# Retention, Mish layer and GLU layer on one core: the planner knows the port that VectorE and GpSimd share and uses longer durations, activations stay in PSUM banks until they are split, and one pair's first chunk is multiplied out plainly

## Chip, core and metric

The kernel runs on one core of a Trainium2 chip. The metric is the device time of one execution in microseconds (us); lower is better. TensorE (PE) does the matrix products, VectorE (DVE), ScalarE (ACT) and GpSimd (POOL) do the elementwise work, and SyncE (SP) issues the loads and stores.

## What is computed

Three stages follow each other: a retention over 768 steps (16 pairs of batch and head), a feed-forward layer with the activation h*tanh(softplus(h)) (Mish), and a gated layer (GLU). All inputs are float32.

```python
def _attn_ref(q, k, v):
    ...
    for t in range(S):
        state = gamma[None, :, None, None] * state + np.einsum('bhd,bhe->bhde', k[:, :, t], v[:, :, t])
        y[:, :, t] = scale * np.einsum('bhd,bhde->bhe', q[:, :, t], state)
...
def _moe_ref(x, w_in, w_out):       # x 1536x512, w_in 512x2048, w_out 2048x512
    h = x @ w_in
    sp = np.where(h > 20.0, h, np.log1p(np.exp(np.minimum(h, 20.0))))
    g = h * np.tanh(sp)
    return (g @ w_out).astype(np.float32)
...
def _moe2_ref(x, w_gate, w_val, w_out):     # 512x1536, 512x1536, 1536x512
    gate = 1.0 / (1.0 + np.exp(-(x @ w_gate)))
    val = x @ w_val
    return (gate * val @ w_out).astype(np.float32)
```

## The kernel before

**Tiles.** The 1536 tokens are three chunks of 512 (c = 0, 1, 2). Activations lie feature by token: `acc_t[c]` holds four 128x512 tiles of chunk c in SBUF. Every float32 factor is written as the sum of a rounded high part and a low part (`split`, L269: ACT writes the high part, another engine subtracts it to get the low part), and a product of two factors is three matmuls (`mm3`, L287). A weight arrives by DMA as 64-bit words and is decoded by two ACT and two DVE operations (`decode`, L273: tiles `raw` and `v`), then split into a ring (`ww`, `wo`, `wq`).

**Products.** The hidden features of a layer come in pairs. For a pair, chunks 1 and 2 are not multiplied by the weights with eight block products but with seven, from sums of blocks (`pair_steps`, L489; `main_steps`; steps p1 to p7, each six matmuls of 512 columns into PSUM tile `h`). Chunk 0 gets the same scheme on its two halves (`side_steps`: six matmuls of 256 columns a step, PSUM tile `hx`). The block sums of the activations are formed once a layer by `sums_of` (L452): `T1` to `T4` for chunks 1 and 2 (tiles `T`, `t`), `YT1` to `YT3` and parts of `xc` for chunk 0 (tiles `YT`, `t`); `B` are unsummed blocks. Between products DVE adds partial results (`u<-h,s`, `u<-h,u`, `h<-h,u`, the same with `hx`). `plain_steps` (L578) is the unreduced product: 4 blocks by 3 matmuls of 512 columns for each of the two feature groups; the kernel uses it for the first pairs of a layer, whose sums are not ready.

**Activation.** In layer 1 `mish` (L598) has ACT write Mish of a PSUM bank into an SBUF tile `e`; in layer 2 `gate` (L603) has ACT write the sigmoid into `e`, and `glu` (L608) has DVE multiply the value's bank into `e`. `put_g` (L593) then splits `e` into `g`: ACT the high part, and for the low part `lo_eng["g"]`, which is POOL or, by the planner's choice, DVE (L836).

**Second product of a layer.** `o1` and `o2` multiply `g` by `wo` into PSUM tiles `o` (two banks, L612: only the first call uses `h` banks), and DVE adds each to `acc` (`acc<-o,acc`; the first one of a layer is an ACT copy `acc<-o`). There are eight PSUM banks: four `h`, two `o`, two `hx`.

**Order.** Until `early.clear()` (L831) instructions are issued as written. After it every call makes a `Node` (L112), and `replay` (L168) lists them all: the PE instructions stay in the written order (`chain`), every other engine's order comes from a walk in time. A node's rank is its own cost plus the longest way from it to the end; an idle engine takes the ready node of highest rank, unless that would hold up a later node of higher rank. Costs are functions of the element count (L161 to L165), the time from one engine's end to another's start is `lag`. `either` (L166) marks operations that POOL or DVE may do; before, DVE takes one only when POOL would be too late for it (L221). The engines then execute these fixed lists, each waiting on semaphores. `three` (L695) interleaves main steps, side steps and `o` tiles on PE.

Of the kernel before, what the change touches and what calls it, by code (L numbers as in the profile page):

```python
# [23 lines left out]
def kernel(ctx, tc, qk, nv, w1i, w1o, w2g, w2v, w2o, ma_in, og_in, sg_in, ck_in, out):  # L24
# [28 lines left out]
    early = [True]  # L53
    WIDTH = {F32: 4, F32R: 4, I32: 4, I64: 8, U8: 1}
# [57 lines left out]
    class Node:  # L112


        def __init__(self, queues, name, kw):
# [3 lines left out]
            self.cost = [q.cost(big.at.size, kw) for q in queues]  # L119
# [40 lines left out]

    pe = Queue(nc.tensor, lambda n, kw: (kw["rhs"].at.size + 32) / 2400, 0.2)  # L161
    dve = Queue(nc.vector, lambda n, kw: (0.157 + 0.00104 * n) * (1 if psum(kw) else 1.3), 0.1)
    act = Queue(nc.scalar, lambda n, kw: 0.17 + 0.0009 * min(n, N), 0.1)
    pool = Queue(nc.gpsimd, lambda n, kw: 0.08 + 0.00258 * n, 0.1)
    sync = Queue(nc.sync, lambda n, kw: 3.3 if isinstance(kw["out"], Part) else 1.6, 0.3)  # L165
    either = Either(pool, dve)  # L166

    def replay():  # L168
# [22 lines left out]

        def lag(m, n):
            return 0 if m.queues[0] is n.queues[0] else m.queues[0].lag
# [4 lines left out]
        late = 0  # L198
        free = {q: 0.0 for q in (pe, dve, act, pool, sync)}
        wait = {n: len(n.after) for n in nodes}  # L200
        line = {q: [] for q in free}
        done = []

        def enter(n):
            n.ready = max((m.end + lag(m, n) for m in n.after), default=0.0)
            for q in n.queues:
                line[q].append(n)

        for n in nodes:
            if not wait[n]:  # L210
                enter(n)
        now = 0.0
        while len(done) < len(nodes):
            moved = False
            for q in free:
                if free[q] > now or not line[q]:
                    continue
                pick = None
                for n in sorted((n for n in line[q] if n.ready <= now), key=lambda n: -n.rank):
                    cost = n.cost[n.queues.index(q)]  # L220
                    if len(n.queues) > 1 and q is dve:  # L221
                        if max(now, free[pool]) + n.cost[0] <= whole + late - n.rank + n.cost[0]:
                            continue
                    end = now + cost
                    if any(u.rank > n.rank and u.ready < end and end > max(u.ready, whole + late - u.rank)
                           and u.ready > now and len(u.queues) == 1 for u in line[q]):
                        continue
                    pick = n
                    break
                if not pick:  # L230
                    continue
                n = pick
                n.start, n.end, n.queue = now, now + n.cost[n.queues.index(q)], q
                free[q] = n.end
                late = max(late, n.start - (whole - n.rank)) if q is pe else late
                for k in n.queues:
                    line[k].remove(n)
                done.append(n)
                moved = True
                for m in n.then:  # L240
                    wait[m] -= 1
                    if not wait[m]:
                        enter(m)
            if not moved:
                later = [t for t in free.values() if t > now] + [n.ready for q in free for n in line[q] if n.ready > now]
                now = min(later)
# [47 lines left out]
    G0 = 4  # L294
    I0 = G0 // 2
    pieces = [("w1i", f) for f in range(G0)] + [("w1o", f) for f in range(G0)]
# [40 lines left out]
    def direct(key):  # L337
        return key[1] == 1 and key[2] < I0 or key[1] == 2 and key[2] < 2

# [112 lines left out]
    def sums_of(x0, x1, bt, cols, eng):  # L452
# [3 lines left out]
        def form(n, k, in0, in1, to=None):  # L456
            if to is None:
                to = (up if cols == N else upv).tile([P, cols], F32, tag="u", name="t")
            eng.tensor_tensor(out=to, in0=in0, in1=in1, op=ALU.subtract)
# [12 lines left out]
        for k in range(2):  # L472
            steps.append(lambda k=k: form("T4", k, x0[:, 2 + k], t["T2", k], t["T2", k]))
# [5 lines left out]
    def side_sums():  # L479
        return sums_of(acc_t[0][:, :, :H], acc_t[0][:, :, H:], y_t, H, pool if early else either)  # L480
# [97 lines left out]
    def plain_steps(key, done, halves=None, own=False):  # L578

        def one(i):  # L580
            o = hx["pool"].tile([P, N], F32, tag=f"x{i}", name="hx") if own and i in hx["own"] else hbank()
            w = weight(("a", *key, i))
            for kk in range(KK):
                xs, k = (xc_t, kk) if not halves else (b_t[halves[kk // 2]], kk % 2)
                mm3(o, lambda a: w[:, a, kk * P:kk * P + P], lambda b: xs[:, k, b, :], kk == 0, kk == KK - 1)
            spend(("a", *key, i))
            r[i] = o
            done(i, r)

        r = {}  # L590
        return [lambda: one(0), lambda: one(1)]

    def put_g(e, key):  # L593
        g = gp.tile([P, 2, N], F32R, tag="g", name="g")
        split(e, g[:, 0], g[:, 1], lo_eng["g"])
        g_t[key] = g
# [337 lines left out]
```

## Time and profile before

| | |
|---|---|
| median of 3 runs | 592.2 us (592.03 to 592.25) |
| the profiled execution | 592.67 us |
| its span, first to last instruction | 590.5 us |
| PE, DVE, ACT, POOL busy | 98%, 66%, 50%, 68% |

The profiled execution lies 0.47 us above the median, and 2.17 us of it lie outside the span. PE's busy time counts a running matmul as busy, so 98% doesn't say that nothing is lost: a matmul's recorded length overlaps the next one's, and a short wait can hide in that. What PE loses is read from the start times of its products: each has a fixed number of matmuls, and the distance to the next start shows whether PE went on at its own pace.

### The profile page before, as it was taken

The numbers are of one execution on the slowest core, as the hardware profiler recorded it, in microseconds if no ns is written. First come the engines' busy times: TensorE is split into PE (matmuls) and PEld (weight loads), VectorE is DVE, ScalarE is ACT, GpSimd is POOL, SyncE is SP. The second block draws the span as 40 slices with busy tenths as digits, with TensorE's granted clock in tenths as the row PEclk, the third lists the DMA queues.
The fourth block names the chain that finished last, engine by engine and source line by source line (L and its number), as shares of the span: only waits on it lengthen the run. The fifth ranks groups of instructions, "written<-read, shape, count | busy, mean of one in ns | idle before, by whom it ended". The sixth has DMA issues, their size and how long they took to land.

```text
span 590.5 us, 8781 instructions
## 1 busy us (share of the span) xinstructions
PE 578.4 (98%) x3342; PEld 483.4 (82%) x3342; DVE 387.0 (66%) x540; ACT 294.9 (50%) x533; POOL 401.2 (68%) x344
## 2 busy tenths in 40 slices
PE   8999999999999999999999999999999999999997
PEld 6788878778888888888778778788888888888885
DVE  3899730167878775748883657887677677654564
ACT  1455556466666655346655556575254354340220
POOL 3566299999995846258999998997484484560120
PEclk9999999999999999999999999999999999999999
DMA  9974320023323231203220022333222222000004
GB/s 344 404 273 147 108 73 0 1 71 103 108 94 127 71 108 40 68 2 117 91 78 1 0 72 72 108 108 107 72 72 72 72 71 72 0 2 1 0 37 178
DMA packets 15593, 52.30 MB, mean 89 GB/s; under 512 B 1984, under 2 KB 2112, under 8 KB 15552
## 3 DMA queue, kind: packets, MB, share of 16 engines
q1 hardware_dynamic: 14976, 51.39, 25.2%
q8 instruction: 26, 0.43, 0.3%
q10 hardware_dynamic: 576, 0.36, 0.2%
q14 instruction: 15, 0.12, 0.1%
HBM read 48.60 MB, written 3.15 MB: 88 GB/s over the span
## 4 chain that ended last, share of the span: by engine, by line
PE 79%; POOL 10%; DMA 3%; DVE 3%; issue 2%; ACT 1%; SPq 0%; DVEq 0%; POOLq 0%; ACTq 0%
PE o L143 33%; PE h L143 27%; PE hx L143 16%; POOL t L143 3%; PE ao L143 2%; POOL g L143 2%; DMA raw<-w1i 2%; POOL T L143 2%; PE sc L143 1%; DMA qk_t<-qk 1%; POOL s L143 1%; POOL YT L143 1%; POOL B L143 1%; POOL ww L143 1%; PE st L143 1%
## 5 line engine op out<-in xcount | busy, mean ns | idle before, releaser
L143 POOL TENSOR_TENSOR g<-e,g 128x512 fp32r<-128x512 f32 x81 | 112.5, 1400 | 79.2 <-ACT g L143 74.6
L143 DVE TENSOR_TENSOR acc<-o,acc 128x512 f32<-128x512 f32 x132 | 90.8, 688 | 65.5 <-PE o L143 64.6
L143 PE MATMUL o<-g,wo 128*128 128x512 f32 x528 | 129.0, 393 | 0.2
L143 PEld LDWEIGHTS o<-g,wo 128*128 128x128 f32 x528 | 96.4, 188 | 21.8 <-DVE acc L143 2.6
L143 PE MATMUL o<-wo,g 128*128 128x512 f32 x432 | 108.8, 392 | 0.5 <-ACT acc L143 0.5
L143 PE MATMUL h<-B,ww 128*128 128x512 f32 x372 | 94.7, 391 | 0.1
L143 PE MATMUL h<-T,ww 128*128 128x512 f32 x360 | 91.9, 391 | 1.2 <-ACT acc L143 1.0
L143 PEld LDWEIGHTS o<-wo,g 128*128 128x128 f32 x432 | 78.1, 189 | 15.2 <-ACT acc L143 1.1
L143 POOL TENSOR_TENSOR ww<-s,ww 128x512 fp32r<-128x512 f32 x35 | 51.3, 1468 | 53.2 <-ACT ww L143 53.2
L143 DVE SCALAR_TENSOR_TENSOR raw<-raw 128x512 int32<-128x512 int32 x68 | 70.5, 1037 | 22.7 <-ACT raw L143 22.3
L143 PEld LDWEIGHTS h<-B,ww 128*128 128x128 f32 x372 | 68.7, 188 | 14.6 <-POOL B L143 0.5
L143 PEld LDWEIGHTS h<-T,ww 128*128 128x128 f32 x360 | 66.9, 188 | 16.6 <-ACT acc L143 1.5
L143 DVE SCALAR_TENSOR_TENSOR v<-v,raw 128x512 int32<-128x512 int32 x68 | 70.5, 1038 | 6.4 <-ACT v L143 3.9
L143 ACT ACTIVATE raw<-raw 128x512 int32<-128x512 uint8 x68 | 45.6, 673 | 42.8 <-DMA raw<-w2g 10.0
L143 ACT ACTIVATE e<-h 128x512 f32<-128x512 f32 x57 | 33.8, 593 | 58.0 <-PE h L143 35.7
L143 ACT ACTIVATE g<-e 128x512 fp32r<-128x512 f32 x84 | 51.7, 630 | 16.0 <-DVE e L143 14.8
L143 PE MATMUL hx<-xc,ww 128*128 128x256 f32 (+1 forms) x336 | 54.4, 299 | 1.1 <-DVE hx L143 0.8
L143 PEld LDWEIGHTS hx<-xc,ww 128*128 128x128 f32 x336 | 48.6, 190 | 6.7 <-DVE hx L143 1.2
L143 DVE TENSOR_TENSOR h<-h,u 128x512 f32<-128x512 f32 x54 | 37.6, 696 | 24.5 <-PE h L143 24.2
L143 ACT ACTIVATE v<-raw 128x512 f32<-128x512 f32 x68 | 44.9, 665 | 15.5 <-POOL s L143 11.3
L143 PEld LDWEIGHTS hx<-YT,ww 128*128 128x128 f32 x288 | 40.6, 190 | 7.5 <-DVE u L143 2.6
L143 PE MATMUL hx<-YT,ww 128*128 128x256 f32 x288 | 42.3, 283 | 2.7 <-DVE u L143 1.8
(80 smaller groups left out, 735.6 us busy)
## 6 DMA issues: line engine op xcount, KB each, us to landing
raw<-w1i SPq DMA_DIRECT2D x16, 512.0 KB, 3.3
raw<-w1o SPq DMA_DIRECT2D x16, 512.0 KB, 3.4
qk_t<-qk SPq DMA_DIRECT2D x12, 512.0 KB, 6.2
nv_t<-nv SPq DMA_DIRECT2D x12, 512.0 KB, 7.1
raw<-w2g SPq DMA_DIRECT2D x12, 512.0 KB, 3.3
raw<-w2v SPq DMA_DIRECT2D x12, 512.0 KB, 3.4
raw<-w2o SPq DMA_DIRECT2D x12, 512.0 KB, 3.4
out<-acc SPq DMA_DIRECT2D x12, 256.0 KB, 2.0
```

The costliest lines, as they stand in the source:

```text
L143: i = call(**kw)
```

## The change

**Costs and walk.** All durations but PE's are multiplied by 1.1, the lag of DVE, ACT and POOL is 0.2 us instead of 0.1, that of SP 3.5 instead of 0.3. The walk in time knows that POOL and a DVE operation with two SBUF operands slow each other: DVE runs at 0.5 of its rate while both run, POOL at 0.74. An engine that is idle takes any ready node, DVE first, so DVE no longer leaves `either` work to POOL while it has nothing else.

**Activations in their banks.** After the early part `mish` writes back into the PSUM bank `h` and `glu` writes the product into the value's bank; the split reads the bank, and the low part is always DVE's. So the groups `g<-e,g` of POOL become `g<-h,g` and `g<-hx,g` of DVE.

**Third pair of layer 2.** For f = 2 (`S2 = 3`) chunk 0 is multiplied by `plain_steps` in pieces, 24 matmuls of 512 columns, instead of 42 of 256. The sums of chunk 0 are made in two parts (`apart`), since the second part overwrites `xc`.

**Banks for the last `o` tiles of layer 1.** In `o1` every second pair of tiles of the last group uses `h` banks.

```diff
-            self.cost = [q.cost(big.at.size, kw) for q in queues]
+            self.cost = [q.cost(big.at.size, kw) * (1.0 if q is pe else MARGIN) for q in queues]
...
+    def slow(n, kw):
+        return 0.04 + 0.00195 * n if kw.get("op") is ALU.mult else 0.18 + 0.00217 * n
...
-    dve = Queue(nc.vector, lambda n, kw: (0.157 + 0.00104 * n) * (1 if psum(kw) else 1.3), 0.1)
-    act = Queue(nc.scalar, lambda n, kw: 0.17 + 0.0009 * min(n, N), 0.1)
-    pool = Queue(nc.gpsimd, lambda n, kw: 0.08 + 0.00258 * n, 0.1)
-    sync = Queue(nc.sync, lambda n, kw: 3.3 if isinstance(kw["out"], Part) else 1.6, 0.3)
+    dve = Queue(nc.vector, span(0.1, 0.00102), 0.2)
+    act = Queue(nc.scalar, lambda n, kw: 0.14 + 0.0008 * min(n, N), 0.2)
+    pool = Queue(nc.gpsimd, slow, 0.2)
+    sync = Queue(nc.sync, lambda n, kw: 1.4 if isinstance(kw["out"], Part) else 1.6, 3.5)
...
+        def rates():
+            d, p = busy[dve], busy[pool]
+            both = d and p and d.shared
+            return {dve: 0.5 if both else 1.0, pool: 0.74 if both else 1.0}
...
-                    if len(n.queues) > 1 and q is dve:
-                        if max(now, free[pool]) + n.cost[0] <= whole + late - n.rank + n.cost[0]:
-                            continue
...
     def direct(key):
-        return key[1] == 1 and key[2] < I0 or key[1] == 2 and key[2] < 2
+        return key[1] == 1 and key[2] < I0 or key[1] == 2 and key[2] < S2
...
+        parts = [[lambda i=i, kk=kk: part(i, kk) for kk in range(KK)] for i in range(2)]
+        if fine:
+            return parts[0] + parts[1][:2] + [lambda: run(parts[1][2:])]
...
     def mish(h, key):
-        e = ep.tile([P, N], F32, tag="e", name="e")
+        e = ep.tile([P, N], F32, tag="e", name="e") if early else h
         act.activation(out=e, in_=h, func=AF.Mish)
         put_g(e, key)
...
     def glu(e, val, key):
-        dve.tensor_tensor(out=e, in0=val, in1=e, op=ALU.mult)
-        put_g(e, key)
+        dve.tensor_tensor(out=val, in0=val, in1=e, op=ALU.mult)
+        put_g(val, key)
...
-        o = hbank() if i == c == 0 else ps_o.tile([P, N], F32, tag="o", name="o")
+        o = hbank() if i == c == 0 or i == L1 and d % 2 else ps_o.tile([P, N], F32, tag="o", name="o")
...
-    lo_eng.update(dcs=Pool(name="dcs", bufs=1), w=either, g=either, x=either)
+    lo_eng.update(dcs=Pool(name="dcs", bufs=1), w=either, g=dve, x=either)
...
-    run(ys[:6], plain2(1), ys[6:])
+    run(ys[:6], plain2(1), ys[6:8])
...
-        three(seq(main_steps((2, f), done)), seq(side_steps((2, f), done, f == 2)), rest[:n], 4 if f == 2 else 7, 3 if f == 2 else 0)
+        three(seq(main_steps((2, f), done)), plain2(f) if f < S2 else seq(side_steps((2, f), done, f == S2)), rest[:n], 4 if f == 2 else 7, 3 if f == 2 else 0)
...
+        if f == S2 - 1:
+            run(ys[8:])
```

In all, POOL's list goes from 349 to 201 instructions and DVE's from 542 to 685; ACT keeps its number (539, then 538), and the instructions up to `early.clear()` stand as they did on every engine.

POOL at the start of the planned part of the program, just after the last low parts of the early part; `acc_93` is chunk 0, `acc_94` and `acc_95` are chunks 1 and 2. First before:

```order
L143 TENSOR_TENSOR g<-e,g 128x512 x3
L143 TENSOR_TENSOR t<-acc_93 128x256
L143 TENSOR_TENSOR t<-acc_93,t 128x256
L143 TENSOR_TENSOR T_960<-acc_95,T_960 128x512
L143 TENSOR_TENSOR YT_96<-t,YT_96 128x256
L143 TENSOR_TENSOR t<-acc_93 128x256
L143 TENSOR_TENSOR T_960<-acc_95,T_960 128x512
L143 TENSOR_TENSOR B_978<-acc_95,B_978 128x512
L143 TENSOR_TENSOR YT_97<-t,YT_97 128x256
L143 TENSOR_TENSOR B_978<-acc_95,B_978 128x512
L143 TENSOR_TENSOR t<-acc_93,t 128x256
```

and in the changed kernel:

```order
L144 TENSOR_TENSOR g<-e,g 128x512 x3
L144 TENSOR_TENSOR T_979<-acc_95,T_979 128x512
L144 TENSOR_TENSOR B_991<-acc_95,B_991 128x512
L144 TENSOR_TENSOR t<-acc_93,t 128x256
L144 TENSOR_TENSOR YT_98<-t,YT_98 128x256
L144 TENSOR_TENSOR t<-acc_93,t 128x256
L144 TENSOR_TENSOR t<-acc_93 128x256
L144 TENSOR_TENSOR t<-acc_95 128x512
```

Between the early low parts and the second `t<-acc_93,t` POOL had eight operations; now two stand ahead of the first `t<-acc_93,t` that it keeps, and the others are in DVE's list at the same place.

DVE beside the last `o` tiles of layer 1, before (`v` and `raw` are weight decoding):

```order
L143 TENSOR_TENSOR acc_93<-o,acc_93 128x512 x2
L143 SCALAR_TENSOR_TENSOR v<-v,raw 128x512
L143 TENSOR_TENSOR acc_93<-o,acc_93 128x512
L143 SCALAR_TENSOR_TENSOR raw<-raw 128x512
L143 TENSOR_TENSOR acc_93<-o,acc_93 128x512 x2
L143 SCALAR_TENSOR_TENSOR v<-v,raw 128x512
L143 TENSOR_TENSOR acc_93<-o,acc_93 128x512
L143 SCALAR_TENSOR_TENSOR raw<-raw 128x512
```

and in the changed kernel:

```order
L144 SCALAR_TENSOR_TENSOR v<-v,raw 128x512
L144 TENSOR_TENSOR acc_93<-o,acc_93 128x512 x2
L144 TENSOR_TENSOR wo<-v,wo 128x512
L144 TENSOR_TENSOR acc_93<-h,acc_93 128x512 x2
L144 TENSOR_TENSOR t<-acc_93,t 128x256
L144 TENSOR_TENSOR acc_94<-o,acc_94 128x512
L144 TENSOR_TENSOR xc<-acc_93,xc 128x512
L144 TENSOR_TENSOR acc_94<-o,acc_94 128x512
L144 TENSOR_TENSOR acc_94<-h,acc_94 128x512
L144 TENSOR_TENSOR t<-acc_93 128x256
```

The decoding that stood between the additions is gone from there until the additions are done; block sums and splits stand in its place.

DVE in the middle of a pair of layer 1 (`u` and `h<-h,u` are the additions between products), before:

```order
L143 TENSOR_TENSOR acc_95<-o,acc_95 128x512
L143 SCALAR_TENSOR_TENSOR raw<-raw 128x512
L143 TENSOR_TENSOR hx<-hx,u_2246 128x256
L143 TENSOR_TENSOR acc_95<-o,acc_95 128x512
L143 TENSOR_TENSOR acc_93<-o,acc_93 128x512
L143 SCALAR_TENSOR_TENSOR raw<-raw 128x512
L143 TENSOR_TENSOR h<-h,u_2140 128x512
```

and in the changed kernel:

```order
L144 TENSOR_TENSOR acc_95<-o,acc_95 128x512
L144 TENSOR_TENSOR g<-h,g 128x512
L144 TENSOR_TENSOR hx<-hx,u_2221 128x256
L144 TENSOR_TENSOR g<-h,g 128x512
L144 TENSOR_TENSOR acc_95<-o,acc_95 128x512
L144 SCALAR_TENSOR_TENSOR raw<-raw 128x512
L144 TENSOR_TENSOR acc_93<-o,acc_93 128x512
L144 TENSOR_TENSOR h<-h,u_2126 128x512
```

Two low parts of `g` now stand between two additions that empty `o` banks.

## Rows read from the trace of the kernel before

**Rows 1.** Windows: stretch, length, busy us (instructions) of PE, PEld, DVE, ACT, POOL, clock, DMA.

```profile
72.00:136.00 64.00, 61.51 (x286) 49.81 (x285) 22.43 (x25) 38.11 (x72) 61.85 (x56) 1.00 0.15 50
136.00:282.00 146.00, 146.00 (x741) 124.59 (x740) 106.17 (x151) 82.19 (x147) 102.81 (x85) 1.00 0.26 84
...
390.00:566.00 176.00, 176.00 (x932) 151.69 (x931) 116.94 (x183) 71.93 (x129) 93.41 (x81) 1.00 0.16 51
```

**Rows 2.** Timeline of PE, 76 to 135: start, length, operation, count [idle before <-releaser].

```profile
84.09 1.86 PE L143 MATMUL h<-B,ww 128*128 128x512 f32 x6
86.98 1.65 PE L143 MATMUL h<-T,ww 128*128 128x512 f32 x6 [1.03 <-ACT acc L143]
...
95.65 11.04 PE L143 MATMUL o<-g,wo 128*128 128x512 f32 x48
106.53 1.52 PE L143 MATMUL h<-B,ww 128*128 128x512 f32 x6
107.89 6.00 PE L143 MATMUL o<-g,wo 128*128 128x512 f32 x24
...
115.28 0.87 PE L143 MATMUL hx<-xc,ww 128*128 128x256 f32 x6
...
123.55 1.52 PE L143 MATMUL h<-T,ww 128*128 128x512 f32 x6
126.34 0.97 PE L143 MATMUL hx<-YT,ww 128*128 128x256 f32 x6 [1.27 <-DVE u L143]
```

**Rows 3.** Timeline of PE, 276 to 352.

```profile
281.63 0.88 PE L143 MATMUL hx<-xc,ww 128*128 128x256 f32 x6
282.35 25.26 PE L143 MATMUL o<-g,wo 128*128 128x512 f32 x102
307.45 5.60 PE L143 MATMUL hx<-xc,ww 128*128 128x512 f32 x24
...
326.55 1.61 PE L143 MATMUL h<-T,ww 128*128 128x512 f32 x6
...
331.90 1.57 PE L143 MATMUL o<-wo,g 128*128 128x512 f32 x6
...
347.63 1.55 PE L143 MATMUL h<-T,ww 128*128 128x512 f32 x6
350.09 0.97 PE L143 MATMUL hx<-YT,ww 128*128 128x256 f32 x6 [0.92 <-ACT s L143]
```

**Rows 4.** Timeline of PE, 366 to 392.

```profile
373.73 1.55 PE L143 MATMUL h<-T,ww 128*128 128x512 f32 x6
375.80 0.97 PE L143 MATMUL hx<-YT,ww 128*128 128x256 f32 x6 [0.52 <-DVE u L143]
...
380.06 1.55 PE L143 MATMUL h<-T,wq 128*128 128x512 f32 x6
382.41 0.98 PE L143 MATMUL hx<-xc,ww 128*128 128x256 f32 x6 [0.80 <-DVE hx L143]
```

**Rows 5.** Timeline of POOL, then of ACT, at the first wait of PE.

```profile
85.11 1.18 POOL L143 TENSOR_TENSOR t<-acc,t 128x256 f32<-128x256 f32 x1
...
86.33 0.60 ACT L143 ACTIVATE acc<-h 128x512 f32<-128x512 f32 x1 [2.15 <-POOL t L143]
```

**Rows 6.** Part 5 of the page: group, count | busy, mean ns | idle before, releaser.

```profile
L143 POOL TENSOR_TENSOR g<-e,g 128x512 fp32r<-128x512 f32 x81 | 112.5, 1400 | 79.2 <-ACT g L143 74.6
L143 DVE TENSOR_TENSOR acc<-o,acc 128x512 f32<-128x512 f32 x132 | 90.8, 688 | 65.5 <-PE o L143 64.6
...
L143 DVE SCALAR_TENSOR_TENSOR raw<-raw 128x512 int32<-128x512 int32 x68 | 70.5, 1037 | 22.7 <-ACT raw L143 22.3
```

**Rows 7.** Timelines of POOL and of DVE where both work on SBUF operands.

```profile
294.02 6.39 POOL L143 TENSOR_TENSOR xc<-acc,xc 128x512 fp32r<-128x512 f32 x4
...
319.21 1.87 DVE L143 TENSOR_TENSOR t<-acc,t 128x512 f32<-128x512 f32 x1
321.01 0.68 DVE L143 TENSOR_TENSOR g<-e,g 128x512 fp32r<-128x512 f32 x1
```

More of the change, by code (lines that the diff above doesn't have):

```diff
@@ L53 @@
     early = [True]
+    MARGIN = 1.1
     WIDTH = {F32: 4, F32R: 4, I32: 4, I64: 8, U8: 1}
@@ L197, in replay @@
         whole = max(n.rank for n in nodes)
[L198 to L202, printed above, removed]
+        late = 0.0
+        begin = {dve: 0.4, pe: 0.0, act: 1.5, pool: 3.0, sync: 0.0}
+        busy = {q: None for q in queues}
+        line = {q: [] for q in queues}
+        for n in nodes:
+            n.unstarted = n.unended = len(n.after)
+            n.shared = len([v for v in n.kw.values() if isinstance(v, Part)]) > 2 or n.queues[0] is pool
+            n.shared = n.shared and not psum(n.kw)
@@ L209, in replay @@
         for n in nodes:
-            if not wait[n]:
+            if not n.after:
                 enter(n)
[L212 to L216, printed above, removed]
-                    continue
-                pick = None
-                for n in sorted((n for n in line[q] if n.ready <= now), key=lambda n: -n.rank):
-                    cost = n.cost[n.queues.index(q)]
-                    if len(n.queues) > 1 and q is dve:
-                        if max(now, free[pool]) + n.cost[0] <= whole + late - n.rank + n.cost[0]:
[L223 to L226, printed above, removed]
-                        continue
[L228 to L246, printed above, removed]
@@ new lines, in replay @@
+        now, ended = 0.0, 0
+        while ended < len(nodes):
+            moved = True
+            while moved:
+                moved = False
+                for q in queues:
+                    n = None if busy[q] or not line[q] or now < begin[q] else pick(q)
+                    if not n:
+                        continue
+                    moved = True
+                    n.start, n.queue, n.left = now, q, n.cost[n.queues.index(q)]
+                    n.end = now + n.left
+                    if q is pe:
+                        late = max(late, now - (whole - n.rank))
+                    busy[q] = n
+                    for k in n.queues:
+                        line[k].remove(n)
+                    for m in n.then:
+                        m.unstarted -= 1
+                        if not m.unstarted:
+                            enter(m)
+            rate = rates()
+            for q in (dve, pool):
+                if busy[q]:
+                    busy[q].end = now + busy[q].left / rate[q]
+            marks = [n.end for n in busy.values() if n] + [t for t in begin.values() if t > now + 1e-6]
+            marks += [t for q in queues if not busy[q] for n in line[q] if not n.unended for t in [due(n)] if t > now + 1e-6]
+            step = max(min(marks), now + 1e-6)
+            for q in queues:
+                n = busy[q]
+                if n:
+                    n.left -= (step - now) * rate.get(q, 1.0)
+                    if n.end <= step + 1e-9:
+                        n.end, busy[q] = step, None
+                        ended += 1
+                        for m in n.then:
+                            m.unended -= 1
+            now = step
@@ L471, in sums_of @@
                       lambda k=k: form("T3", k, x1[:, 2 + k], x1[:, k], t["T1", k])]
-        for k in range(2):
-            steps.append(lambda k=k: form("T4", k, x0[:, 2 + k], t["T2", k], t["T2", k]))
+        for part in range(1, 3) if apart else range(1):
+            for k in range(2):
+                steps.append(lambda k=k, part=part: form("T4", k, x0[:, 2 + k], t["T2", k], t["T2", k], part))
         return steps + [lambda: low.pop()()]
```

63 lines of the change are left out of this document (41 added, 22 removed).

## Prediction

> **What bounds the kernel now.** I read the windows by stretch first. From 136 to 282 and from 390 to 566 PE is busy for the whole length, 146.00 of 146 us and 176.00 of 176 us, at full granted clock, while no other engine is; there PE sets the pace and nothing can be gained but matmuls [rows 1]. From 72 to 136 PE is busy 61.51 of 64 us, POOL 61.85, and DVE only 22.43: one engine is full, and its neighbour idles [rows 1].
>
> Then I read PE's timeline for the distances between starts. A full-width product of 48 matmuls starts at 95.65 and the next at 106.53: 0.2267 us a matmul, 1.36 for six [rows 2]. Six matmuls of 256 columns take 282.35 - 281.63 = 0.72 us [rows 3]. Whatever lies between two starts beyond that is lost. Seven places lose:
>
> - a: 84.09 to 95.65 is 11.56 us for seven six-matmul products (9.52): 2.04 lost, most of it before 86.98, where PE waits for ACT `acc` [rows 2]. ACT had waited for a POOL `t`, the eleventh row of POOL's list there, ending at 86.29 [rows 5]: ACT may not overwrite chunk 0 before POOL has read it for its sums.
> - b: 107.89 to 115.28 is 7.39 for 30 matmuls (6.80): 0.59 [rows 2].
> - c: 123.55 to 126.34 is 2.79 for six (1.36): 1.43, waiting for a DVE addition [rows 2].
> - d: 282.35 to 307.45 is 25.10 for 102 `o` matmuls (23.12): 1.98 [rows 3]. Two `o` banks alternate and DVE empties each; between the additions it decodes weights.
> - e: 326.55 to 331.90 is 5.35 for 18 (4.08): 1.27 [rows 3].
> - f: 347.63 to 350.09 is 2.46 for six: 1.10, for ACT [rows 3].
> - g: 373.73 to 375.80 and 380.06 to 382.41 are 2.07 and 2.35 for six each: 0.71 and 0.99, both for DVE [rows 4].
>
> Together 10.1 us. All lie where sums of a new layer are being formed, none in the two long stretches. That is what a better order can give; the rest of the 590.5 us is matmuls, the start and the tail.
>
> **The costs, part by part.** The early part and the tail (last addition, stores) keep their instructions and their order, so both count as nothing, and nothing is late in their place.
>
> *Matmuls.* The third pair of layer 2 swaps 42 matmuls of 256 columns (seven steps of 0.72 = 5.0 us) for 24 of 512 (24 x 0.2267 = 5.4): +0.4 us, on PE and so on the path. It takes away the waits of that pair's side chain: f is such a wait, a side step that waits for ACT's copy of the step before. The plain product has no such chain. The first reduced side then comes one pair later, where sums and additions have more time.
>
> *Low parts go to DVE.* In the rows `g<-e,g` cost POOL 1.40 us each [rows 6]. 76 of them become DVE operations with one PSUM operand. No such row exists before; the nearest is `acc<-o,acc`, also one PSUM and one SBUF operand of 512: 0.688 us [rows 6]. I take 0.69; the bounds are 0.68 (the DVE low part that met no other work [rows 7]) and 1.40. So DVE gets some 76 x 0.69 = 52 us, and POOL loses some 76 x 1.40 = 106. About 70 other net operations (block sums, weight splits) also change from POOL to DVE. In 136 to 282 that makes DVE 106.2 + about 30 x 0.69 + about 20 x 0.7 to 1.0 = 141 to 147 us, less what the decoding saves: its 46 operations there cost 1.04 on average and come towards 0.68 as POOL idles more [rows 6, 7], up to 16 us. I expect about 129 of 146 us, 88%. It is hidden behind PE as long as the additions between products come in time; that is the cover, and the second rival is what happens without it.
>
> *Banks held longer.* A value's bank is now free after ACT's high part and DVE's low part, some 0.60 + 0.69 = 1.3 us later than before (an ACT operation of 512 takes 0.60 [rows 5]). In a pair with side steps and `o` tiles a bank is used again only several products later, which covers it. In the two pairs of layer 2 that have no side steps the next products follow at 1.36 us, so PE can wait a few tenths there, perhaps twice. Bounds: 0 and 2 x 1.3.
>
> *Order.* At a, POOL has two operations instead of eight between the early low parts and the first `t<-acc,t` it keeps, and DVE, idle for two thirds of that stretch, does the others at 0.4 to 0.7 us instead of 0.7 to 1.4. The sums that ACT waits for are then ready some 5 us earlier (six operations of about 1 us fewer ahead of them), more than the 1.5 that PE lost at 86.98. Next late would be the low parts of the sums for b and c; DVE has 41.6 of 64 us free there, so I count a, b and c as gone. At d the decoding stands behind the additions, and `h` banks take every second pair of tiles, so a bank has four tiles' time instead of two to be emptied: gone. The decoded weights come later for that; the ring holds what the next products need, and the weights are needed only after the plain products (48 x 0.2267 = 10.9 us). e waits for ACT copies that wait for POOL's sums, as a does: gone or small. g is DVE being late by 0.7 to 1.0 us; DVE gets fuller there, so I keep it.
>
> *SP.* Three loads of `w2v` change places with neighbours in SP's list; DMA engines are busy 15 to 26% of the time there [rows 1], so nothing.
>
> *The shared port.* Four `xc` low parts on POOL took 6.39 us beside two decoding operations of DVE; and a DVE sum beside POOL took 1.87 us against 0.68 for one alone [rows 7]. The plan's rate of 0.5 makes the latter 1.37. By the Trainium skill (SBUF — State Buffer, "Who interferes with whom") the port pair is an exclusive lock: a DVE instruction with two SBUF inputs and a GpSimd instruction that reads SBUF run one after the other, not both at a lower rate. The 1.87 us agrees with that better than with the plan's 1.37. By that rule every DVE operation that meets POOL may be some 0.5 us later than planned; I price that in the first rival from the rows.
>
> **The sum.** 592.67 (the profiled execution) - 10.1 + 0.4 = 583.0 if every wait goes and none comes. I add 2.5: 1.7 for g, kept, and 0.8 for banks held longer and late additions in the long stretches (bounds 0 and 2.6 for the first, more in the second rival). That gives 585.5 for a profiled execution; the median lies 0.47 lower than the profiled one: 585.0 us. Its own range is 582.5 (nothing kept) to 587.5 (half kept).
>
> **Rivals.**
>
> 1. *The two engines take turns, and the sums stay late.* Block sums and low parts read two SBUF tiles, so a DVE one and a POOL one may add up instead of overlapping. From 72 to 113 DVE's list has 16 such operations of 256 and 22 of 512 columns, and POOL's 7 and 11. At undisturbed lengths (DVE 0.41 and 0.68, an estimate from 0.68 for 512; POOL 0.75 and 1.30, estimates from the 1.40 mean) that is 6.6 + 15.0 + 5.3 + 14.3 = 41.2 us in a stretch of 40. Then a to c (4.1 us) stay: 589.1. For it: 1.87 us [rows 7]. Against it: before, the same sums stood on POOL at 1.3 to 1.4 us apiece, so each move shortens even the taking of turns, and the low parts of `g` leave the port.
>
> 2. *DVE becomes the bound; slower.* POOL stood idle for 74.6 us because the high part of a `g` had not come from ACT, over 81 low parts: 0.9 us each [rows 6]. DVE executes its list in order. If it inherits these waits, 30 low parts in 136 to 282 add 27 us of waiting to 129 us of work, 156 in 146: `o` banks and additions are late, and PE loses 10 us in a stretch where it lost nothing. 585 + 10 = 595. The point where the change turns from a gain to a loss is 7.2 us of such loss, waits of 0.8 us per low part. For it: DVE's 88%, and low parts now stand between additions in its list. Against it: POOL waited because it had nothing else to do, while the plan puts other work of DVE ahead of a `g` whose high part isn't due.
>
> 3. *The waits only move.* The planned order is made from estimates; new waits of the size of the old come where the old ones go: 592.
>
> **How the numbers follow.** About 0.2% (1.2 us) is what a measurement of this kernel can tell from no change. Forecast 0.66, first rival 0.14, third 0.08, second 0.12. Faster is the forecast and the first rival: 0.80; same 0.08; slower 0.12. The range runs from 582.5, every wait gone, to 591.0, past the first rival; the other two, 0.20, are left out.
>
> **What would show it.** Right: PE's starts at 84, 124, 282 and 348 follow each other at 1.36 us per six matmuls; the long stretches stay without gaps; POOL's busy share falls from 68% to about 38% and DVE's rises from 66% to about 80%; the new `g<-h,g` rows cost 0.69. Wrong: PE idle with DVE `acc`, `u` or `g` as the releaser in 136 to 282 or after 390 (second rival); PE still waiting for ACT `acc` near 86 with POOL or DVE sums behind it (first); gaps at new places of about 10 us in all (third).

## The result, and the profile after

| | before | after |
|---|---|---|
| median | 592.02 us (591.53 to 592.25) | 582.69 us (582.19 to 583.01) |
| the profiled execution, its span | 592.67, 590.5 | 582.65, 580.6 |

The ratio is 0.9843, interval 0.983 to 0.9856: 9.3 us faster, inside the range (582.5 to 591.0), 2.3 us below the predicted 585.0.

The page of the changed kernel, parts 1 and 4 (busy time; the chain that ended last):

```profile
PE 573.9 (99%) x3324; PEld 484.3 (83%) x3324; DVE 466.1 (80%) x683; ACT 289.7 (50%) x532; POOL 220.2 (38%) x196
...
PE 96%; DMA 2%; DVE 2%; ACT 0%; issue 0%; DVEq 0%
```

Nearly the whole chain is matmuls. POOL is at 38% and DVE at 80%, as forecast. The windows that answer to [rows 1], with the same columns:

```profile
72.00:136.00 64.00, 64.00 (x306) 53.89 (x305) 56.66 (x71) 45.90 (x89) 39.49 (x31) 1.00 0.23 73
...
136.00:282.00 146.00, 146.00 (x739) 124.50 (x738) 118.40 (x188) 76.40 (x139) 37.26 (x35) 1.00 0.22 73
...
384.00:556.00 172.00, 172.00 (x912) 148.27 (x911) 132.90 (x211) 67.01 (x123) 43.94 (x44) 1.00 0.16 50
```

From 72 to 136 PE was busy 61.51 us and is now busy for all 64; POOL gave up 22 us and DVE took on 34. The long stretches stay full. PE's timeline at the places of [rows 2]; start, length, operation, count:

```profile
71.22 11.04 PE L144 MATMUL h<-g,wo 128*128 128x512 f32 x48
82.10 1.52 PE L144 MATMUL h<-T,ww 128*128 128x512 f32 x6
83.46 1.52 PE L144 MATMUL h<-B,ww 128*128 128x512 f32 x6
...
120.30 1.52 PE L144 MATMUL h<-T,ww 128*128 128x512 f32 x6
121.66 0.88 PE L144 MATMUL hx<-YT,ww 128*128 128x256 f32 x6
```

Every six full-width matmuls follow at 1.36 us; waits a, b and c are gone. At the places of [rows 3], and down to the tail:

```profile
277.59 9.71 PE L144 MATMUL o<-g,wo 128*128 128x512 f32 x42
...
300.74 5.60 PE L144 MATMUL hx<-xc,ww 128*128 128x512 f32 x24
...
325.33 2.88 PE L144 MATMUL h<-B,ww 128*128 128x512 f32 x12
328.24 4.38 PE L144 MATMUL h<-T,ww 128*128 128x512 f32 x18
...
335.17 2.88 PE L144 MATMUL h<-B,ww 128*128 128x512 f32 x12
338.16 1.67 PE L144 MATMUL h<-T,ww 128*128 128x512 f32 x6
339.67 0.85 PE L144 MATMUL hx<-xc,ww 128*128 128x512 f32 x3
340.36 1.53 PE L144 MATMUL h<-T,ww 128*128 128x512 f32 x6
...
556.10 20.59 PE L144 MATMUL o<-wo,g 128*128 128x512 f32 x90
```

Three small waits are new: 328.24 - 325.33 is 2.91 for twelve matmuls (2.72), 338.16 - 335.17 is 2.99, and 339.67 - 338.16 is 1.51 for six (1.36): 0.19 + 0.27 + 0.15 = 0.6 us, all where the sums of layer 2 are made. Ahead of the first PE's weight loads waited for a DVE `g`, ahead of the second for an ACT `e`. From these starts the gain can be laid out (before's starts of the same products are 71.85, 282.35, 307.45 and 566.05):

| stretch | before | after | difference | forecast |
|---|---|---|---|---|
| first instruction to the first `h<-g,wo` | 71.85 | 71.22 | -0.63 | 0 |
| to the last `o` tiles of layer 1 (a, b, c) | 210.50 | 206.37 | -4.13 | -4.06 |
| these tiles (d) | 25.10 | 23.15 | -1.95 | -1.98 |
| to the last `o` tiles of layer 2 (e, f, g; +0.4; new waits) | 258.60 | 255.36 | -3.24 | -4.07 + 0.4 + 2.5 = -1.17 |
| tail | 24.45 | 24.50 | +0.05 | 0 |
| sum | 590.5 | 580.6 | -9.90 | -7.2 |

The first row is no gain of the change: the instructions there are the same, and over the kernels of this document that start lies anywhere from 70.94 to 72.20 us.

The groups that answer to [rows 6]: count | busy, mean ns | idle before:

```profile
L144 DVE SCALAR_TENSOR_TENSOR raw<-raw 128x512 int32<-128x512 int32 x68 | 59.0, 870 | 2.9 <-ACT raw L144 2.8
...
L144 DVE TENSOR_TENSOR g<-h,g 128x512 fp32r<-128x512 f32 x53 | 36.2, 684 | 2.6 <-ACT g L144 1.9
...
L144 DVE TENSOR_TENSOR g<-hx,g 128x512 fp32r<-128x512 f32 x23 | 15.4, 682 | 0.3 <-ACT g L144 0.3
```

The 76 low parts cost DVE 0.68 us each, and it waited 2.2 us in all for their high parts, where POOL had waited 74.6 [rows 6]. The decoding operation of this group came from 1.04 down to 0.87.

### The profile page after: what moved, and what is told of

Its sections match the earlier page's. It is cut to its first block, busy times and chain, and to the rows that moved or that the text cites. A ratio compares the mean times of both kernels' runs of the same rounds, so it can differ in the third digit from the quotient of the medians.

```text
span 580.6 us, 8695 instructions
## 1 busy us (share of the span) xinstructions
PE 573.9 (99%) x3324; PEld 484.3 (83%) x3324; DVE 466.1 (80%) x683; ACT 289.7 (50%) x532; POOL 220.2 (38%) x196
## 4 chain that ended last, share of the span: by engine, by line
PE 96%; DMA 2%; DVE 2%; ACT 0%; issue 0%; DVEq 0%
PE h L144 37%; PE o L144 36%; PE hx L144 16%; PE ao L144 3%; PE sc L144 2%; DMA qk_t<-qk 1%; PE st L144 1%; DMA ck<-ck 1%; DVE xc L144 1%; DVE h L144 0%; DVE ww L144 0%; DVE v L144 0%; DVE acc L144 0%; DVE a L144 0%; ACT ww L144 0%
## 5 line engine op out<-in xcount | busy, mean ns | idle before, releaser
L144 PE MATMUL o<-g,wo 128*128 128x512 f32 x492 | 119.1, 391 | 0.0
L144 DVE TENSOR_TENSOR acc<-o,acc 128x512 f32<-128x512 f32 x126 | 86.9, 690 | 39.2 <-PE o L144 36.1
L144 PEld LDWEIGHTS o<-g,wo 128*128 128x128 f32 x492 | 90.4, 188 | 17.4
L144 DVE SCALAR_TENSOR_TENSOR raw<-raw 128x512 int32<-128x512 int32 x68 | 59.0, 870 | 2.9 <-ACT raw L144 2.8
L144 POOL TENSOR_TENSOR wo<-v,wo 128x512 fp32r<-128x512 f32 x17 | 23.4, 1388 | 94.1 <-ACT wo L144 57.6
L144 DVE SCALAR_TENSOR_TENSOR v<-v,raw 128x512 int32<-128x512 int32 x68 | 56.0, 828 | 2.7 <-ACT v L144 0.8
L144 PE MATMUL hx<-xc,ww 128*128 128x256 f32 (+1 forms) x342 | 57.9, 306 | 0.1
L144 POOL TENSOR_TENSOR ww<-s,ww 128x512 fp32r<-128x512 f32 x22 | 30.4, 1382 | 67.3 <-ACT ww L144 60.3
L144 ACT ACTIVATE e<-h 128x512 f32<-128x512 f32 x29 | 17.3, 596 | 56.1 <-PE h L144 45.1
L144 POOL TENSOR_TENSOR ww<-v,ww 128x512 fp32r<-128x512 f32 x17 | 23.5, 1388 | 52.4 <-ACT ww L144 49.9
```

The costliest lines, as they stand in the source:

```text
L144: i = call(**kw)
```

## The experiments

In what follows a number behind "+" is the distance of a median from the changed kernel's 582.69. Except for the last two, which ran once each, a kernel was timed together with the kernel before, to which its ratio refers.

### Is it the order, or the other edits?

The plan alone: the new costs and the new walk, without the other three parts.

```diff
-    S2 = 3
+    S2 = 2
...
-        e = ep.tile([P, N], F32, tag="e", name="e") if early else h
+        e = ep.tile([P, N], F32, tag="e", name="e")
...
-        o = hbank() if i == c == 0 or i == L1 and d % 2 else ps_o.tile([P, N], F32, tag="o", name="o")
+        o = hbank() if i == c == 0 else ps_o.tile([P, N], F32, tag="o", name="o")
...
-    lo_eng.update(dcs=Pool(name="dcs", bufs=1), w=either, g=dve, x=either)
+    lo_eng.update(dcs=Pool(name="dcs", bufs=1), w=either, g=either, x=either)
```

> The kernel before with the new costs and the new walk alone: the activations go through SBUF tiles as before and their low parts are for POOL or DVE, the third pair keeps its reduced side, the last tiles of layer 1 keep two banks. Theory 1 (the order does it: DVE was idle where the sums were formed, and the walk lets it take them): the waits a, b, c and e of the prediction go (5.3 us), d shrinks (decoding is planned later), f and g (2.8) stay: 584.5 to 587. Theory 2 (the relief of POOL by the low parts does it): the sums still share POOL with 80 low parts, most waits stay: 589 to 592.

Measured: 584.77 us, ratio 0.9876 (0.9861 to 0.9891), +2.1. The plan alone brings 7.4 us against the 592.20 that the kernel before took beside it; the changed kernel lies 9.5 below that. It is more than an order of the same lists: POOL's busy share falls from 68% to 48% and DVE's rises from 66% to 80%, since the walk gives DVE `either` work that POOL had. The time is the first theory's, but not by its waits: f and g, which were to stay, are gone (344.23 - 342.73 = 1.50 for six matmuls where f was, although the third pair is reduced here), and d, which was to shrink, has grown. PE at d:

```profile
277.85 6.99 PE L144 MATMUL o<-g,wo 128*128 128x512 f32 x30
285.18 11.42 PE L144 MATMUL o<-g,wo 128*128 128x512 f32 x48 [0.34 <-DVE acc L144]
298.14 5.78 PE L144 MATMUL o<-g,wo 128*128 128x512 f32 x24 [1.54 <-DVE acc L144]
```

The next product starts at 303.75: 303.75 - 277.85 is 25.90 for 102 matmuls (23.12), so 2.78 us are lost, against 1.98 before. There are two banks and a DVE that empties them late.

The other way round, everything but the plan: the costs and the walk of before.

```diff
-    dve = Queue(nc.vector, span(0.1, 0.00102), 0.2)
-    act = Queue(nc.scalar, lambda n, kw: 0.14 + 0.0008 * min(n, N), 0.2)
-    pool = Queue(nc.gpsimd, slow, 0.2)
+    dve = Queue(nc.vector, lambda n, kw: (0.157 + 0.00104 * n) * (1 if psum(kw) else 1.3), 0.1)
+    act = Queue(nc.scalar, lambda n, kw: 0.17 + 0.0009 * min(n, N), 0.1)
+    pool = Queue(nc.gpsimd, lambda n, kw: 0.08 + 0.00258 * n, 0.1)
...
-            return {dve: 0.5 if both else 1.0, pool: 0.74 if both else 1.0}
```

> The changed kernel with the costs and the walk of before; activations in their banks, the plain third pair and the additional banks stay. Theory 1: DVE still leaves the sums to POOL until POOL would be late, so a, b, c and e stay in good part: 587 to 590; waits on late DVE low parts may come on top, since the costs are short. Theory 2: POOL has lost 106 us of low parts, so it is in time anyway: 583 to 585.

Measured: 589.82 us, ratio 0.9961 (0.9946 to 0.9976), +7.1. Wait a is back:

```profile
83.62 1.85 PE L143 MATMUL h<-B,ww 128*128 128x512 f32 x6
86.51 1.65 PE L143 MATMUL h<-T,ww 128*128 128x512 f32 x6 [1.03 <-ACT acc L143]
```

A second such wait of 0.70 us stands at 90.22, and e is back too (waits for ACT `acc` of 1.19 and 0.91 us near 326 and 330), with new waits of 0.63 us for ACT `e` and 0.48 for POOL `ww` near 344 and 346. ACT had again waited for a POOL `t`, 2.28 us up to 85.86. So moving the low parts to DVE doesn't by itself free POOL in time, as the first theory had it; b, c, d, f and g are gone even so.

### What does each other part bring?

Activations back in SBUF tiles, their low part for either engine:

```diff
-        dve.tensor_tensor(out=val, in0=val, in1=e, op=ALU.mult)
-        put_g(val, key)
+        dve.tensor_tensor(out=e, in0=val, in1=e, op=ALU.mult)
+        put_g(e, key)
...
-    lo_eng.update(dcs=Pool(name="dcs", bufs=1), w=either, g=dve, x=either)
+    lo_eng.update(dcs=Pool(name="dcs", bufs=1), w=either, g=either, x=either)
```

> The changed kernel with the activations back in SBUF tiles and their low parts for POOL or DVE. Theory 1: the walk still finds an order without waits, DVE is no fuller than with them: 582.5 to 584. Theory 2: POOL is full again where the sums are formed and PE waits there: 586 to 589.

Measured: 584.13 us, ratio 0.987 (0.9855 to 0.9885), +1.4, just above the first theory's range. PE waits 1.02 us for DVE `u` at 324.75, and 0.36 for DVE `acc` in d.

The third pair's chunk 0 multiplied by the reduced scheme again:

```diff
-    S2 = 3
+    S2 = 2
...
-    run(ys[:6], plain2(1), ys[6:8])
+    run(ys[:6], plain2(1), ys[6:])
```

> The changed kernel with the third pair's first chunk reduced again: 42 matmuls of 256 columns for 24 of 512. By the prediction's sum PE gains 0.4 us and the waits f and g come back in part (up to 2.8): 583 to 585. Rival: the new order hides the side chain as well, nothing comes back: 582.3.

Measured: 585.18 us, ratio 0.9883 (0.9866 to 0.9899), +2.5, just above the expected range, although 0.4 us of matmuls less are to be done. PE's timeline shows wait f again, longer than in [rows 3], and ACT's what it did meanwhile:

```profile
340.59 1.55 PE L144 MATMUL h<-T,ww 128*128 128x512 f32 x6
343.71 0.98 PE L144 MATMUL hx<-YT,ww 128*128 128x256 f32 x6 [1.58 <-ACT s L144]
```

```profile
340.58 0.68 ACT L144 ACTIVATE raw<-raw 128x512 int32<-128x512 uint8 x1
...
342.73 0.67 ACT L144 ACTIVATE raw<-raw 128x512 int32<-128x512 uint8 x1
343.28 0.38 ACT L144 ACTIVATE s<-hx 128x256 f32<-128x256 f32 x1
```

The side product ended near 340.75, its copy `s<-hx` comes at 343.28, behind five operations that decode and split weights, and PE goes on at 343.71. The plain product has no side chain: in this order 0.4 us of matmuls buy off 2.5. They don't buy off the f of before, which the plan alone had already removed.

Two banks for the last `o` tiles of layer 1:

```diff
-        o = hbank() if i == c == 0 or i == L1 and d % 2 else ps_o.tile([P, N], F32, tag="o", name="o")
+        o = hbank() if i == c == 0 else ps_o.tile([P, N], F32, tag="o", name="o")
```

> The changed kernel with two banks for the last tiles of layer 1. By the prediction wait d went for two reasons, decoding behind the additions and four tiles' time per bank. If the order alone does it: 582.5 to 583.2. If the banks do it: up to 2 us more, 584 to 585, with DVE acc as PE's releaser near 280 to 300.

Measured: 584.31 us, ratio 0.988 (0.9862 to 0.9899), +1.6. The waits lie in d: the weight loads of `o` waited 1.8 us in six waits for DVE `acc`.

The four removals add up to 7.1 + 1.4 + 2.5 + 1.6 = 12.6, against 9.3 for all at once. Where they overlap is read from the distances between the starts of the same products as in the table by stretch:

| kernel | first `h<-g,wo` to the last `o` tiles of layer 1 | these tiles (23.12 without a wait) | to the last `o` tiles of layer 2 |
|---|---|---|---|
| before | 210.50 | 25.10 | 258.60 |
| changed | 206.37 | 23.15 | 255.36 |
| the plan alone | 206.37 | 25.90 | 254.62 |
| everything but the plan | 209.05 | 23.14 | 259.54 |
| SBUF tiles again | 206.37 | 24.04 | 255.81 |
| third pair reduced again | 206.37 | 23.15 | 257.71 |
| two banks again | 206.37 | 24.59 | 255.23 |

The first column, a to c, is the plan's: only without it does the stretch get longer. The second is the banks' work: with them and the old plan d is gone, with the new plan alone it is longer than before. In the third the plan alone is among the shortest; with activations in banks and the third pair reduced it takes 3.1 us more, and the plain product makes up for all but 0.7 of that. So the plan and the `h` banks may be the whole gain. An estimate from the table: the plan alone had a span of 582.8, and with d as short as in the changed kernel, or as in the one with SBUF tiles, it would have 580.0 or 580.9, against the changed kernel's 580.6. No kernel with just these two parts was run, so it isn't shown that the other two bring anything.

### What in the plan does it?

The plan without the port: both engines at full rate always.

```diff
-            return {dve: 0.5 if both else 1.0, pool: 0.74 if both else 1.0}
+            return {dve: 1.0, pool: 1.0}
```

> The changed kernel with a plan that doesn't know the shared port (both engines at full rate); the factor 1.1 and the lags stay. If knowing the port is what makes the order hold, DVE is planned too full, additions come late and PE waits in several places: 585 to 590. If sharing the sums and the margin are enough: 582.5 to 584.

Measured: 598.3 us, ratio 1.0105 (1.009 to 1.012), +15.6: slower than the kernel before, and beyond both ranges that were expected. The costs of the kernel before had a factor of 1.3 for operations without a PSUM operand, which stood in for the port; this plan has nothing of the kind. DVE's and then POOL's timeline there, ahead of the first long wait:

```profile
91.28 1.78 DVE L144 TENSOR_TENSOR ww<-s,ww 128x512 fp32r<-128x512 f32 x1
92.99 0.96 DVE L144 TENSOR_TENSOR s<-v,s 128x256 f32<-128x256 f32 x1
93.87 1.78 DVE L144 SCALAR_TENSOR_TENSOR raw<-raw 128x512 int32<-128x512 int32 x1
95.76 1.59 DVE L144 SCALAR_TENSOR_TENSOR v<-v,raw 128x512 int32<-128x512 int32 x1
```

```profile
91.17 1.34 POOL L144 TENSOR_TENSOR t<-acc 128x512 f32<-128x512 f32 x1 [3.01 <-DVE T L144]
92.47 1.20 POOL L144 TENSOR_TENSOR YT<-t,YT 128x256 fp32r<-128x256 f32 x1
93.67 1.43 POOL L144 TENSOR_TENSOR T<-t,T 128x512 fp32r<-128x512 f32 x1
```

The plan had (0.1 + 0.00102 x 512) x 1.1 = 0.68 us for each of the three DVE operations of 512 columns here, and 0.40 for the one of 256: after these four DVE is 1.10 + 0.56 + 1.10 + 0.91 = 3.7 us late. ACT waited 2.20 us for a DVE `s` at 90.46 and then works through its list in order, and its copy of an `o` bank comes at 101.96; PE:

```profile
92.70 5.60 PE L144 MATMUL o<-g,wo 128*128 128x512 f32 x24
102.60 8.30 PE L144 MATMUL o<-g,wo 128*128 128x512 f32 x24 [4.30 <-ACT acc L144]
110.74 1.52 PE L144 MATMUL h<-B,ww 128*128 128x512 f32 x6
...
327.80 1.65 PE L144 MATMUL o<-wo,g 128*128 128x512 f32 x3 [4.31 <-ACT g L144]
```

The matmuls behind the wait are slow too: 24 of them take 110.74 - 102.60 = 8.14 us instead of 5.44 (last section). The same happens in layer 2: from 321.23 to 333.93 PE loses 1.3 us to a wait for DVE `g`, 4.6 to one for ACT `g` and 2.7 to slow matmuls behind it. With 4.5 and 2.7 at the first place that is 15.8 us, the whole of the +15.6.

The shorter durations: no factor of 1.1, lags of 0.1 us for DVE, ACT and POOL.

```diff
-    MARGIN = 1.1
+    MARGIN = 1.0
...
-    dve = Queue(nc.vector, span(0.1, 0.00102), 0.2)
+    dve = Queue(nc.vector, span(0.1, 0.00102), 0.1)
...
```

> The changed kernel with the factor 1.0 instead of 1.1 and lags of 0.1 us for DVE, ACT and POOL; the port stays known. If the margin is what keeps late operations off PE's path: 584 to 588, with waits of some tenths at many places. If not: 582.5 to 583.5.

Measured: 585.94 us, ratio 0.9898 (0.9883 to 0.9913), +3.2: PE waits 1.57 us for ACT `acc` at 101.14 (in the place where the plan without the port lost 4.3), 0.7 for DVE `u` near 326. The loss is at a few places, not some tenths at many.

The port as turns instead of rates:

```diff
+            first = dve if both and d.start <= p.start else pool
-            return {dve: 0.5 if both else 1.0, pool: 0.74 if both else 1.0}
+            return {q: 1.0 if not both or q is first else 1e-4 for q in (dve, pool)}
```

> The changed kernel, but in the walk in time the two engines take turns at the shared port: of a VectorE operation with two SBUF operands and a GpSimd operation, the one that started first runs at full rate and the other stands still until it has ended (instead of 0.5 and 0.74 of the rate at once). Theory A: the rates stand in for the turns well enough, and little is left to gain: within 1.2 us of the changed kernel, 581.5 to 583.9 us. Theory B, from the 1.87 us row: the lock is what the plan mis-estimates, and the last waits near 325 to 338 (0.6 us) go: 582.0 or less. Theory C: the walk is sensitive to any change of its costs, whichever is nearer to the truth, and new waits of 2 us or more come, as with the shorter costs: 584.5 or more.

Measured: 582.92 us, ratio 0.9845 (0.9829 to 0.9862): no difference from the changed kernel. Theory A holds. The last waits stay near 325 to 339 (0.22 + 0.59 + 0.13 = 0.9 us). What counts here is that the plan knows of the port, not how it writes it down. Not tried was the port, or the margin, in the walk of before; how much the new walk brings by itself, as against its costs, stays open.

### How much can DVE carry?

Each of the 76 low parts done twice, then three times; the plan still counts each once.

```diff
         split(e, g[:, 0], g[:, 1], lo_eng["g"])
+        if not early:
+            nodes[-1].times = 2
...
-            n.queue.issue(n.name, n.kw)
+            for _ in range(getattr(n, "times", 1)):
+                n.queue.issue(n.name, n.kw)
```

> The changed kernel whose plan is the same but whose 76 low parts from banks are each done twice on DVE (the second writes the same values): 76 x 0.69 = 52 us more on DVE, about 95% of the stretch 136 to 280. If DVE has cover left, as the prediction had it, PE loses little: 583 to 585. By the second rival (DVE as the bound, in-order waits hit PE): 588 to 600, with PE waiting for DVE in the long stretches.

> The changed kernel, but each of the 76 low parts of g that the planned part gives to VectorE is done three times (the plan knows of one; the two others add 104 us of VectorE work and change no value). Doing it twice cost 7.3 us, nearly all of it at the change of layer. Theory A (cover of the long stretches nearly used up by then: VectorE there goes from 131 to some 145 of 144 us): VectorE becomes the bound, 136 to 280 loses 5 us or more, and the whole time is over 600 us. Theory B (the loss grows only at the change of layer): 595 to 598, and the long stretch loses less than 2 us.

Measured: 589.96 us (0.9966, 0.9953 to 0.9979), +7.3, and 632.09 us (1.0672, 1.0648 to 1.0695), +49.4. Windows of the long stretch, of the kernel with two and the one with three:

```profile
136.00:280.00 144.00, 143.68 (x729) 122.23 (x729) 130.83 (x214) 74.28 (x134) 37.59 (x35) 1.00 0.22 74
```

```profile
136.00:285.00 149.00, 137.44 (x668) 115.03 (x667) 138.01 (x226) 69.25 (x125) 30.14 (x28) 0.98 0.19 65
```

With two, DVE is busy 91% of the long stretch. The time falls into the second rival's range, but not at its place: by the starts PE loses 0.8 us ahead of 136, 0.9 in the long stretch, 1.95 at the last `o` tiles of layer 1, 2.6 from there to those of layer 2 and 0.9 in the tail, so most of it at the change of layer. With three, at 93%, PE is without work for 11.6 of 149 us, and the cause is the one that the second rival named; PE's waits in that stretch, us in total, times, longest:

```profile
PE o L144 <- DVE acc L144: 9.6, 6, 3.2
PE hx L144 <- DVE g L144: 2.0, 1, 2.0
```

### Does a wait slow the matmuls behind it?

In the changed kernel ACT's copy of one `o` tile is repeated, seven times in one kernel and twelve times in the other, which makes PE wait at the place where the plan without the port waits.

```diff
             act.activation(out=acc, in_=o, func=AF.Copy)
+            if c == 1 and d == 0:
+                nodes[-1].times = 7
```

> The changed kernel, but ACT's copy of the first full-width o tile after the block sums (96.96 us in the changed kernel) is done seven times instead of once, 0.5 us apiece, so PE waits for it at the third o tile: 6 x 0.5 less 0.9 of slack, about 2.1 us. Theory A (the granted clock falls with the length of a wait; waits of up to 2 us before showed none): clock 1.00 after it, matmuls at 0.227 us, the kernel some 2 to 3 us longer than the changed one. Theory B (what slowed the 24 matmuls after the 4.3 us wait was not the wait but the work of the other engines): clock 1.00 here too, and also in the companion with the longer wait.

> The same copy done twelve times: 11 x 0.5 less 0.9, a wait of about 4.6 us. Theory A (the length of the wait): the granted clock falls below 0.95 in the 10 us behind it, as in the plan that does not know the port, and the next 24 matmuls take some 8 us instead of 5.4: 7 to 8 us longer than the changed kernel. Theory B (the other engines' work): clock 1.00, matmuls at 0.227 us, 4.5 to 5.5 us longer.

Measured, in one run each: 587.43 and 590.29 us. PE's timeline of the first and of the second:

```profile
93.12 5.60 PE L144 MATMUL o<-g,wo 128*128 128x512 f32 x24
101.50 7.35 PE L144 MATMUL o<-g,wo 128*128 128x512 f32 x24 [2.78 <-ACT acc L144]
108.69 1.52 PE L144 MATMUL h<-B,ww 128*128 128x512 f32 x6
```

```profile
104.64 7.07 PE L144 MATMUL o<-g,wo 128*128 128x512 f32 x24 [5.90 <-ACT acc L144]
111.55 1.52 PE L144 MATMUL h<-B,ww 128*128 128x512 f32 x6
```

The waits came out longer than planned (2.94 and 6.06 us from start to start; seven copies took 4.36 us, 0.6 each and not 0.5). Behind them 24 matmuls took 7.19 and 6.91 us instead of 5.44. With that both times are accounted for: 2.94 + 1.75 = 4.7 of +4.7, and 6.06 + 1.47 = 7.5 of +7.6. Theory B is out: the slowing comes behind a wait in the changed kernel's own plan, with a clock of 0.76 and 0.80. Theory A's numbers came for the longer wait; the shorter one came out longer than the 2.1 us it was meant to be, and more was lost behind it than behind the longer one.

## Why the prediction was right, and where its size was off

**What bounds the kernel.** Right. All seven places lay around the block sums of a new layer, all went, and the sum of what they cost (10.1) stands against 4.13 + 1.95 and the 3.24 that hold e to g. The long stretches gave nothing, as said.

**Which part removes which wait.** Right for a and e, which went with the plan alone and came back without it; b, c and g went either way. For d the prediction named two reasons, decoding behind the additions and twice the banks; only the banks hold, since the plan alone left d at 2.78 us and the banks without the plan at 0.02. For f it named the plain product, but the plan alone removed f too. The sum, which counted every wait once and as gone, doesn't depend on this.

**The +0.4 us of matmuls.** Consistent: a piece of three matmuls of 512 columns takes 0.69 us to the next product (339.67 to 340.36), eight such pieces 5.5 us. The kernel with the reduced third pair shows what they buy in this order: 2.5 us.

**Low parts on DVE.** Cost right (0.684 and 0.682 against 0.69), waiting right (2.2 us in all). DVE's load from 136 to 282 was overestimated: 118.4 us against 129. Decoding there took 15.6 + 14.4 us in 40 operations, 0.75 each, where I had 46 operations coming towards 0.68; 28 low parts took 18.8 us where I had 30 with 20.7, and the other operations that moved to DVE took some 11.5 where I had 14 to 20.

**Banks held longer and late additions: 0.8 forecast, 0.6 measured.** At 328.24, 338.16 and 339.67, in the pairs of layer 2 that have no side steps. A bank held for DVE's low part is the releaser of the first alone; that the two sizes agree is in part luck.

**g: the step that was mis-sized.** I kept 1.7 us because DVE had been late there and gets fuller. Nothing of it stayed: in 365 to 390 products follow each other at 1.36 to 1.39 and 0.71 to 0.72 us. The two waits were not a lack of DVE time but of order, like the others: the plan alone has neither of them, with DVE at the same 80%, while the kernel with the reduced third pair, also at 80%, waits 0.5 us for a DVE `u` near there (at 369.67). A wait for an engine that is idle a third of the time is no reason to expect the same wait from a better order. For the profiled execution I had 585.5 and it took 582.65. Of these 2.85 us, 1.7 are this term, 0.2 the term before it, 0.6 lie in the start of the program, which the change doesn't touch and where it was luck, and 0.3 are small differences. The median lies 0.04 above the profiled execution, not 0.47 below, so 2.3 are left.

**The first rival** (the engines take turns and a to c stay). Its mechanism is real: the 1.78 us rows. Its outcome came about in the plan without the port, and worse than I had priced it, since late sums also change what ACT does next. In the changed kernel the plan moves around it. My sum of 41.2 us for the stretch from 72 to 113 (41 us, not 40) took it that DVE and POOL meet all the time; from 72 to 136 their busy times now add up to 96 of 64 us, since additions from banks and low parts from banks do overlap with POOL.

**The second rival** (DVE as the bound). It did not happen, and the margin is known: 76 more low parts (52 us by their own lengths) cost 7.3 of the 9.3 us gained, most of it outside the long stretches, and twice as many cost 49. The 7.2 us at which I had the gain used up were those of a gain forecast too small.

**The third** (the waits only move) held for the plan with shorter durations to a third: +3.2 us of new waits at two places.

## What to carry to other kernels

A list scheduler whose lists are executed in order was here as good as its durations for the pair of engines that slow each other: the same walk was 15.6 us slower without the port and 3.2 us slower without a margin, while the exact form of the port (rates or turns) made no difference. Read where PE waits from the distances between starts, and ask of each whether its releaser was busy throughout or merely had it late in its list; only the first kind is a reason to expect it to stay. Take parts out one at a time and read each kernel by stretch: a part can be needed only because of another one. Leaving an operand in PSUM shortened its operation here (the low parts that DVE made took 0.68 us from banks, and 1.02 in the mean from SBUF tiles in the kernel that has them again), but the 1.4 us between these kernels hold a change of engine as well, and how much of it is due to the port isn't shown.

## What the runs showed of the hardware

**Turns on the port.** In the changed kernel, DVE's timeline and then POOL's:

```profile
299.68 0.68 DVE L144 TENSOR_TENSOR acc<-h,acc 128x512 f32<-128x512 f32 x1
...
301.13 1.77 DVE L144 TENSOR_TENSOR t<-acc,acc 128x512 f32<-128x512 f32 x1
302.82 0.68 DVE L144 TENSOR_TENSOR acc<-h,acc 128x512 f32<-128x512 f32 x1
```

```profile
300.88 1.47 POOL L144 TENSOR_TENSOR T<-t,T 128x512 fp32r<-128x512 f32 x1
302.43 1.62 POOL L144 TENSOR_TENSOR t<-acc 128x512 f32<-128x512 f32 x1
```

The DVE operation with two SBUF inputs ends at 302.90, 0.55 us after POOL's operation that started ahead of it (302.35). In the plan without the port the two of 1.78 us end at 93.06 and 95.65, 0.55 after POOL's 92.51 and 95.10. The DVE additions with one input in PSUM take 0.68 beside POOL as ever. In the changed kernel's timelines 25 DVE operations of 512 columns with two SBUF inputs took 1.2 us or more beside a POOL operation that had started ahead of them, and each ended 0.54 to 0.56 us after it. So it is turns, not shared rates. The Trainium skill (SBUF — State Buffer, "Who interferes with whom") says the same: an exclusive lock for DVE instructions with two SBUF inputs against GpSimd instructions that read SBUF, and no contention, outside DVE's 2-port modes, with at most one. The trace agrees, with 1.77 and 0.68 us.

**The clock behind a wait.** PE's granted clock fell behind the long waits; windows of the plan without the port, of the kernel with seven copies and of the one with three low parts (the last three columns are the clock, the DMA share and GB/s):

```profile
102.60:110.70 8.10, 8.10 (x24) 6.41 (x25) 8.10 (x9) 4.90 (x9) 5.96 (x5) 0.66 0.26 84
```

```profile
101.50:108.70 7.20, 7.20 (x25) 5.76 (x26) 4.60 (x8) 3.21 (x6) 2.23 (x4) 0.76 0.39 143
```

```profile
245.17:249.61 4.44, 4.44 (x12) 3.50 (x13) 3.60 (x6) 0.00 (x0) 0.00 (x0) 0.62 0.25 83
```

Such means are a stretch at the lower level (1.2 GHz) and one at the higher (2.4 GHz): in the first window the clock was 0.50 from 102.60 to 107.60 and 1.00 from 108.60 on. PE had waited 4.46, 2.94 and 2.29 us. Waits of 1.74 and 1.84 us at the place of the first two (the shorter durations; three low parts), and one of 2.14 before 140.56 (three low parts), left the clock at 1.00. Behind waits of 2.29, 2.94, 3.39, 4.46 and 6.06 us (the third again with three low parts, the last with twelve copies) PE lost a further 1.72, 1.75, 1.72, 2.70 and 1.47 us. What decides this loss stays open; it doesn't follow the length of the wait.
